# A two-block kernel (global filter by DFT, then an MLP mixer): filter loads spread over three queues, the rounding's addition on Pool, the first token weights folded in two halves, and the next batch's head between a batch's last products

## Chip, cores, metric

One core of a Trainium2 chip. The metric is the device time of one execution in microseconds, as a median of several runs of the same kernel. Kernels that were timed together ran on the same chip. A ratio is the mean time of one kernel's runs over that of the other's of the same rounds, so it is not quite the ratio of the medians quoted beside it. Engines are written as the profile has them: PE (matmul), PEld (weight load), DVE, ACT, POOL, SP; "SPq" and "ACTq" are DMA issues of those engines.

## The reference

```python
X = np.fft.rfft(x, axis=1)                                # x: (8, 3008, 256)
y = np.fft.irfft(X * (filt_r + 1j * filt_i)[None], n=3008, axis=1).astype(np.float32)
xt = y.transpose(0, 2, 1)
h = np.maximum(xt @ w_tok1, 0) @ w_tok2                   # token mixing, 3008 -> 256 -> 3008
u = y + h.transpose(0, 2, 1)
out = (u + np.maximum(u @ w_ch1, 0) @ w_ch2).astype(np.float32)   # channels, 256 -> 1536 -> 256
```

The four weights arrive as float64 and are rounded to float32 on the chip.

## The kernel before

Before the matmul work of batch 0 can run at full rate there are three stages. **A**: twelve units of the first DFT of batch 0, beside them twelve pieces of the first token weights, each rounded on ACT and DVE and then *folded* with the inverse DFT on PE. **B**: sixteen chunks of two units each: second DFT, product with the filter on DVE, inverse DFT. **C**: sixteen roundings of the second token weights. After that PE works on the mixer of a batch, with the DFT of the following batches between. The parts that the change touches:

```python
def filt_load(c):                      # nine (for c = 0: twelve) DMAs, all on SP
    for src, i, p0 in ((filt_r, 0, 0), (filt_r, 0, HALF), (filt_i, 1, HALF)):
        nc.sync.dma_start(...)         # and two reversed pieces
# filt_keep(c): the arranged filter goes to DRAM;  filt_again(c): later batches fetch it with two DMAs

def rounded(st, n, parts):             # float64 words in st -> float32
    top, rest = pp.tile(...), pp.tile(...)                     # two buffers each
    nc.scalar.activation(out=top, in_=hi_f, func=AF.Copy, scale=2.0 ** -112)
    nc.vector.tensor_scalar(out=top_i, ...)                    # shift
    nc.vector.scalar_tensor_tensor(out=top_i, in0=hi, ...)     # sign
    nc.vector.tensor_scalar(out=rest_i, in0=top_i, ...)        # exponent
    nc.vector.scalar_tensor_tensor(out=rest, in0=lo, ...)
    for src, dst in parts:
        nc.vector.tensor_tensor(out=dst, in0=src(top), in1=src(rest), op=ALU.add)

# ... main part
for i, _ in enumerate(dft(GROUPS[0])):
    if i < A // 2:
        next(convert)                  # rounding i; then the load of a later piece, on POOL
    if 0 < i <= A // 2:
        w1_fold(i - 1)                 # the fold of the step before
# ... 16 + 2 further roundings, then mix(b): token_hidden, u of part 0, 36 items of products
```

In the stretches of the traces that were read here each engine runs its instructions in the order in which the program emits them; a DMA issue waits in its engine's order like any other.

Of the kernel before, what the change touches and what calls it, by code (L numbers as in the profile page):

```python
# [17 lines left out]
B = 8  # L18
N = 3008
N1 = 47  # L20
N2 = 64
# [92 lines left out]
def kernel(  # L114
# [24 lines left out]
    f_d = nc.dram_tensor("f_tmp", (K2 // KC, P, 2, KC, D), FP32, kind="Internal").ap()  # L139

# [41 lines left out]
    def filt_load(c):  # L182
        t, k0 = filts[c % FB], c * KC
        for src, i, p0 in ((filt_r, 0, 0), (filt_r, 0, HALF), (filt_i, 1, HALF)):
            nc.sync.dma_start(t[p0:p0 + A, i], raw(src, k0, [[64 * D, A], [D, KC], [1, D]]))
            lo = p0 + 32
            if k0 == 0:
                nc.sync.dma_start(t[lo:lo + A, i, 0, :], raw(src, 32, [[64 * D, A], [1, D]]))
            k = max(k0, 1)

            for j0, n in ((0, 16), (16, A - 1 - 16)):
                nc.sync.dma_start(t[lo + j0:lo + j0 + n, i, k - k0:KC, :],  # L192
                                  raw(src, 64 * (j0 + 1) - k, [[64 * D, n], [-D, k0 + KC - k], [1, D]]))

    def filt_parts(c):
        t = filts[c % FB]
        return (t[:, 0], f_d[c, :, 0]), (t[HALF:P, 1], f_d[c, HALF:P, 1])

    def filt_keep(c):
        for sb, dr in filt_parts(c):  # L200
            nc.sync.dma_start(dr, sb)

    def filt_again(c):
        for sb, dr in filt_parts(c):
            nc.sync.dma_start(sb, dr)
# [3 lines left out]
    stages = ([(t4p, "t4")] * (A // 2) + [(up, "u")] * 2  # L209
              + [((t2p, "t2"), (t3p, "t3"))[i % 2] for i in range(TC * N2 // NG + JT - 2)])  # L210
# [5 lines left out]
    def rounded(st, n, parts):  # L216

        words = [st.bitcast(t).rearrange("p (n w) -> p n w", w=2)[:, 0:n] for t in (U32, FP32)]
        lo, hi, hi_f = words[0][:, :, 0], words[0][:, :, 1], words[1][:, :, 1]

        top = pp.tile([P, 512], FP32, tag="p1", name="top")[:, 0:n]
        rest = pp.tile([P, 512], FP32, tag="p2", name="rest")[:, 0:n]
        top_i, rest_i = top.bitcast(U32), rest.bitcast(U32)


        nc.scalar.activation(out=top, in_=hi_f, func=AF.Copy, scale=2.0 ** -112)
        nc.vector.tensor_scalar(out=top_i, in0=top_i, scalar1=3, scalar2=None, op0=ALU.logical_shift_left)
        nc.vector.scalar_tensor_tensor(out=top_i, in0=hi, scalar=0x80000000, in1=top_i,  # L228
                                       op0=ALU.bitwise_and, op1=ALU.bitwise_or)
        nc.vector.tensor_scalar(out=rest_i, in0=top_i, scalar1=0xFF800000, scalar2=None, op0=ALU.bitwise_and)  # L230

        nc.vector.scalar_tensor_tensor(out=rest, in0=lo, scalar=2.0 ** -52, in1=rest, op0=ALU.mult, op1=ALU.mult)  # L232
        for src, dst in parts:
            nc.vector.tensor_tensor(out=dst, in0=src(top), in1=src(rest), op=ALU.add)
# [41 lines left out]
    def wc1_load(i):  # L276
        c, q = divmod(i, DC // 512)
        st = stage(512)
        for g in range(CB):
            nc.gpsimd.dma_start(st[ts(g, CW)], moe_w_ch1[ds((g * DH + c) * CW, CW), ts(q, 512)])  # L280
        yield
        rounded(st, 512, [(lambda v: v, wc1[:, c, ts(q, 512)])])

    def wc2_load(i):
        st = stage(512)
        nc.gpsimd.dma_start(st.rearrange("p (j d) -> p j d", d=D),
                            moe_w_ch2[ts(i, 2 * P), :].rearrange("(j p) d -> p j d", p=P))
        yield

        def tile_of(dh):  # L290
            return lambda v: v.rearrange("p (j g e i) -> p e j g i", j=2, e=DH, i=CW)[:, dh]

        a11, a12, s4, na22, s3, s2, s1 = (wc2[:, i, n, :] for n in range(7))

        rounded(st, 512, [(tile_of(dh), wc2[:, i, n].rearrange("p j (g i) -> p j g i", i=CW))
                          for dh, n in ((0, slice(0, 2)), (1, slice(4, 7, 2)))])
        add = nc.gpsimd.tensor_tensor
        nc.gpsimd.tensor_scalar(out=na22, in0=s1, scalar1=-1.0, scalar2=None, op0=ALU.mult)
        add(out=s1, in0=s3, in1=s1, op=ALU.add)
        add(out=s3, in0=a11, in1=s3, op=ALU.subtract)  # L300
        add(out=s2, in0=s1, in1=a11, op=ALU.subtract)
        add(out=s4, in0=a12, in1=s2, op=ALU.subtract)  # L302
# [5 lines left out]
    def weights():  # L308

        steps = ([w1_load(i) for i in range(A // 2)] + [w2_load(i) for i in range(TC * N2 // NG)]  # L310
                 + [wc1_load(c * (DC // 512)) for c in range(DH)]
                 + [f(i) for f, i in LAST])
        n1 = A // 2
        for s in steps[0:AHEAD]:
            next(s)
        yield
        for i, s in enumerate(steps[0:n1]):
            next(s, None)
            if i + AHEAD < n1 + 2:
                next(steps[i + AHEAD])  # L320
            yield
        for s in steps[n1 + 2:n1 + AHEAD]:
            next(s)
        for i, s in enumerate(steps[n1:]):
            next(s, None)
            if n1 + i + AHEAD < len(steps):
                next(steps[n1 + i + AHEAD])
# [26 lines left out]
    def dft(bs):  # L354
# [12 lines left out]
        def load(c):  # L367
# [6 lines left out]
            if first:  # L374
                filt_load(c)
                if c:
                    filt_keep(c - 1)
            else:
                filt_again(c)
# [38 lines left out]
        for k in range(K2 + 1):  # L418
# [6 lines left out]
            if k == K2 and first:  # L425
                filt_keep(K2 // KC - 1)
# [74 lines left out]
    def finish(b, m, ut, po):  # L501
# [24 lines left out]
        for h in range(2):  # L526
            n = min(4, (w - h * HALF + HALF) // P)
            for e in range(2):
                for g in range(CB):
                    nc.gpsimd.dma_start(rows[g, e, :, ds(h * A + 4 * m, n)], blocks[ts(g, CW), h, e, 0:n])  # L530

    def mix(b, next_ready, convert):
        h1 = token_hidden(b)
        wait = []
        uts, pos, hhs, sms = {}, {}, {}, {}

        def u_part(m, dh):
            if dh == 0:
                uts[m] = up.tile([P, DH, 512], FP32, tag="u", name="u")
            u_unit(b, m, h1, uts[m], dh)  # L540
            if dh == DH - 1 and b + 1 < B:
                wait.append(m)

        def step():
            if next_ready():
                for c in wait:
                    t4_load(b + 1, c)
                wait.clear()

        for dh in range(DH):  # L550
            u_part(0, dh)
        items = [(m, jp) for m in range(MT) for jp in range(JP)]
        for i in range(len(items) + 1):
            for half in range(2):
                next(convert, None)
                if i < len(items):
# [3 lines left out]
                    hidden(uts[m], 2 * jp + half, width(m), hhs[i])  # L560
                    if half == 1:
                        sms[i] = sums(hhs[i], width(m))
                        if m + 1 < MT and jp in (2, 3):
                            u_part(m + 1, jp - 2)
                if half == 1 and i >= 1:
                    m, jp = items[i - 1]
                    products(m, jp, hhs.pop(i - 1), sms.pop(i - 1), pos.setdefault(m, []))
                    if jp == JP - 1:
                        finish(b, m, uts[m], pos[m])
                step()  # L570
                yield

    with tc.manual_schedule():
# [5 lines left out]
        next(convert)  # L579
        for i, _ in enumerate(dft(GROUPS[0])):  # L580
# [3 lines left out]
            if i < A // 2:  # L584
                next(convert)
            if 0 < i <= A // 2:
                w1_fold(i - 1)
        for c in range(A // TC4):
            t4_load(0, c)
        for _ in range(TC * N2 // NG + DH):  # L590
            next(convert)
        for bs, after in zip(GROUPS, GROUPS[1:] + ((),)):
# [41 lines left out]
```

## Time and profile before

| | before |
|---|---|
| median of 4 runs | 2755.6 us (2750.8 to 2756.4) |
| PE busy | 95% |
| A: first product of B starts | 65.1 us |
| B: its last product starts | 174.5 us |
| C: second token weights ready | 221.2 us |
| first mixer product (`ps_pg`) | 231.0 us |
| last product ends / span ends | 2733.5 / 2752.2 us |

The prediction below quotes the views that carry the reading: busy shares, slices, stretches, the ring of stage A, the SP queue of stage B and the waits of PE. Two more views belong to it. First the engine table cut at the ends of B and C (length, then busy time of PE, PEld, DVE, ACT and POOL with the number of instructions, granted clock, DMA share, GB/s):

```profile
65.11:175.62 110.51, 63.56 (x129) 33.11 (x127) 53.37 (x128) 11.99 (x32) 1.25 (x3) 0.55 0.61 177
176.47:221.25 44.78, 23.46 (x96) 19.96 (x96) 42.01 (x97) 9.33 (x17) 10.99 (x21) 0.73 0.73 238
```

In B no compute engine is full; SP's issues take 5.8 of each 6.9 us (the prediction shows them). In C DVE is busy 42.0 of 44.8 us. One rounding of C in the timeline (start, length, engine and line, operation, the idle time before it):

```profile
177.43 0.55 DVE L228 SCALAR_TENSOR_TENSOR top<-st,top 128x376 uint32<-128x376 uint32 x1
...
178.98 0.86 DVE L234 TENSOR_TENSOR w<-top,rest 128x368 f32<-128x368 f32 x2
```

The two additions take 0.86 us together.

### The profile page before, as it was taken

What the parts mean: (1) busy time and instruction counts of PE and PEld (TensorE: products, weight loads), DVE (VectorE), ACT (ScalarE), POOL (GpSimd) and SP (SyncE); (2) the same over time, 40 slices, a digit from 0 to 9 for tenths busy, and PEclk for the clock granted to TensorE, in tenths of its full rate; (3) what the DMA queues carried; (4) which work ended last, traced back from release to release, by engine and by line L of the source; (5) the groups of instructions that cost most, each with busy time, mean ns of one, the idle gap of its engine ahead of it and who ended that gap; (6) DMA issues with size and microseconds to landing.
All of it is one profiled execution on the core that took longest, in us unless ns stands there. A gap on an engine that the chain in (4) does not pass through costs nothing.

```text
span 2752.2 us, 25374 instructions
## 1 busy us (share of the span) xinstructions
PE 2609.9 (95%) x9112; PEld 1677.0 (61%) x9112; DVE 1213.1 (44%) x2306; ACT 529.0 (19%) x941; POOL 471.7 (17%) x873
## 2 busy tenths in 40 slices
PE   4567999999999999999999999999999999999997
PEld 1344655576666666675666665676666766676665
DVE  5468377522336356322235455431345343323333
ACT  3113222112222122112221112211212111111111
POOL 2014211121121112121112111210211211221122
PEclk9568999999999999999999999999999999999998
DMA  7665344412233222202232222211322211000000
GB/s 220 182 210 173 123 141 128 130 34 87 76 101 93 63 88 63 82 15 84 83 108 78 67 87 74 71 31 59 99 73 76 69 47 31 23 15 8 8 16 15
DMA packets 163140, 222.31 MB, mean 81 GB/s; under 512 B 29764, under 2 KB 100967, under 8 KB 163015
## 3 DMA queue, kind: packets, MB, share of 16 engines
q1 hardware_dynamic: 92519, 126.90, 15.4%
q0 software_dynamic: 29760, 43.31, 6.3%
q10 hardware_dynamic: 40736, 50.48, 5.4%
q8 instruction: 73, 1.20, 0.2%
q14 instruction: 52, 0.43, 0.1%
HBM read 139.30 MB, written 81.26 MB: 80 GB/s over the span
## 4 chain that ended last, share of the span: by engine, by line
PE 91%; DVE 3%; DMA 3%; SPq 1%; issue 1%; ACT 1%; POOL 0%; ACTq 0%; DVEq 0%; POOLq 0%
PE ps_pg L467 35%; PE ps_po L498 31%; PE ps_acc L455 6%; PE ps_acc L441 5%; PE ps_b L386 4%; PE ps_acc L402 4%; PE ps_acc L460 3%; PE ps_b L349 3%; DMA t<-z_tmp 1%; DMA g_tmp<-t 1%; SPq L192 0%; DVE top L228 0%; DVE rest L232 0%; DMA wai_t<-wait_t 0%; DVE rest L230 0%
## 5 line engine op out<-in xcount | busy, mean ns | idle before, releaser
L467 PE MATMUL ps_pg<-u,wc 128*128 128x512 f32 (+1 forms) x2304 | 1046.9, 584 | 0.0
L530 POOL DMA_DIRECT2D out_dram<-r x768 | 416.0, 550 | 2047.5 <-DVE r L523 1943.6
L467 PEld LDWEIGHTS ps_pg<-u,wc 128*128 128x128 f32 x2304 | 436.4, 190 | 421.3 <-issue 401.7
L469 ACT ACTIVATE hh<-ps_pg 128x512 f32<-128x512 f32 (+1 forms) x576 | 338.8, 588 | 1512.9 <-PE ps_pg L467 1512.9
L498 PE MATMUL ps_po<-t,wc 128*128 128x256 f32 (+1 forms) x2304 | 582.4, 375 | 0.0
L482 DVE TENSOR_TENSOR t<-hh 128x512 f32<-128x512 f32 (+1 forms) x288 | 195.7, 679 | 875.0 <-ACT hh L469 873.9
L498 PEld LDWEIGHTS ps_po<-t,wc 128*128 128x128 f32 x2304 | 438.4, 190 | 50.0
L498 PE MATMUL ps_po<-hh,wc 128*128 128x256 f32 (+1 forms) x1728 | 461.1, 376 | 2.2 <-POOL wc L302 2.2
L498 PEld LDWEIGHTS ps_po<-hh,wc 128*128 128x128 f32 x1728 | 322.3, 190 | 119.4 <-issue 88.4
L394 DVE TENSOR_TENSOR p<-ps_b,filt 128x512 f32<-128x512 f32 (+1 forms) x144 | 86.2, 598 | 368.9 <-PE ps_b L386 329.6
L455 PE MATMUL ps_acc<-w,h 128*128 128x512 f32 (+1 forms) x384 | 180.5, 593 | 25.8 <-ACT h L444 19.5
L386 PE MATMUL ps_b<-t,wb 96*128 96x512 f32 (+1 forms) x288 | 137.0, 559 | 48.2 <-DMA t<-z_tmp 33.7
L441 PE MATMUL ps_acc<-t,w 128*128 128x256 f32 x768 | 169.6, 383 | 8.7 <-DMA t<-g_tmp 8.7
L441 PEld LDWEIGHTS ps_acc<-t,w 128*128 128x128 f32 x768 | 147.6, 192 | 29.5 <-issue 9.4
L402 PE MATMUL ps_acc<-p,wi 128*96 128x512 f32 (+1 forms) x320 | 152.8, 562 | 5.1 <-issue 2.8
L462 DVE COPY u<-ps_acc 128x512 f32<-128x512 f32 (+1 forms) x96 | 65.3, 680 | 195.4 <-PE ps_acc L460 194.0
L455 PEld LDWEIGHTS ps_acc<-w,h 128*128 128x128 f32 x384 | 72.1, 191 | 113.6 <-issue 82.8
L407 ACT COPY t<-ps_acc 96x512 f32<-96x512 f32 (+1 forms) x160 | 79.5, 497 | 286.4 <-PE ps_acc L402 286.4
L460 PEld LDWEIGHTS ps_acc<-wai,t 128*128 128x128 f32 x768 | 101.4, 192 | 44.8 <-issue 44.8
L484 DVE TENSOR_TENSOR t<-t,hh 128x256 f32<-128x256 f32 (+1 forms) x288 | 121.4, 421 | 9.9
L483 DVE TENSOR_TENSOR t<-t,hh 128x256 f32<-128x256 f32 (+1 forms) x288 | 120.8, 419 | 9.8
L386 PEld LDWEIGHTS ps_b<-t,wb 96*128 96x128 f32 x288 | 56.6, 203 | 112.0 <-issue 47.7
(50 smaller groups left out, 1160.5 us busy)
## 6 DMA issues: line engine op xcount, KB each, us to landing
z_tmp<-t ACTq DMA_DIRECT2D x96, 256.0 KB
t<-z_tmp SPq DMA_DIRECT2D x128, 192.0 KB
g_tmp<-t ACTq DMA_DIRECT2D x128, 192.0 KB
t<-g_tmp SPq DMA_DIRECT2D x48, 512.0 KB
x<-in_x_dram SPq DMA_DIRECT2D x176, 128.0 KB
out_dram<-r POOLq DMA_DIRECT2D x704, 32.0 KB, 1.8
filt<-f_tmp SPq DMA_DIRECT2D x64, 256.0 KB
filt<-f_tmp SPq DMA_DIRECT2D x64, 128.0 KB
```

The costliest lines, as they stand in the source:

```text
L386: nc.tensor.matmul(ps, wbs[k // WC][:, k % WC, :], t2s[k // KC][:, k % KC], start=True, stop=True)
L402: nc.tensor.matmul(ps[0:KR], wis[k // WC][:, k % WC, :], prods.pop(k), start=True, stop=True)
L441: nc.tensor.matmul(acc[:, t, :], w1[:, a, ts(t, P)], t4[b, a // TC4][:, a % TC4, :], start=(a == 0 and t == 0), stop=(a == A - 1 and t == ...
L455: nc.tensor.matmul(ps[:, 0:w], h1[:, t, ts(dh, P)], w2[:, t, ds(m * 512, w)], start=(t == 0), stop=False)
L460: nc.tensor.matmul(ps[:, ds(q * P, n)], t4[b, c][:, r, ts(dh, P)], wai[:, 0:n], start=False, stop=(q == 3))
L467: nc.tensor.matmul(ps[:, 0:w], wc1[:, c, ts(jt, P)], ut[:, c, 0:w], start=(c == 0), stop=(c == DH - 1))
L469: nc.scalar.activation(out=hh[:, jt % 2, 0:w], in_=ps[:, 0:w], func=AF.Relu)
L482: v(out=t[:, 0:2, 0:hw], in0=hh[:, :, hw:w], in1=hh[:, 0, 0:w].rearrange("p (s n) -> p s n", s=2), op=ALU.subtract)
L483: v(out=t[:, 2, 0:hw], in0=t[:, 1, 0:hw], in1=hh[:, 0, 0:hw], op=ALU.add)
L484: v(out=t[:, 3, 0:hw], in0=t[:, 2, 0:hw], in1=hh[:, 1, 0:hw], op=ALU.subtract)
L498: nc.tensor.matmul(po[i][:, j, 0:hw], wc2[:, jp, n, :], mov, start=(jp == 0 and j == 0), stop=(jp == JP - 1 and j == len(parts) - 1))
L530: nc.gpsimd.dma_start(rows[g, e, :, ds(h * A + 4 * m, n)], blocks[ts(g, CW), h, e, 0:n])
```

## The change

Its intent: take SP's issues out of stage B, take the additions off DVE, spread the token weights' folding over A and B, fill PE's waits at the batch boundaries, and issue the last outputs from three queues. The core of the diff:

```diff
-    def filt_load(c):
+    def filt_load(c, queues):
...
+        for q, (src, i, p0) in zip(queues, ((filt_r, 0, 0), (filt_r, 0, HALF), (filt_i, 1, HALF))):
+            q.dma_start(...)
-            if first: filt_load(c); if c: filt_keep(c - 1)      # shortened
-            else: filt_again(c)
+            filt_load(c, (nc.sync, nc.scalar, nc.gpsimd) if first else (nc.sync,) * 3)
+    early = [(up, "u")] * 2 + [(tp, "t")] * 2 + [(rp, "r")] * 2   # staging of w2: other pools than t2, t3
...
-            nc.vector.tensor_tensor(out=dst, in0=src(top), in1=src(rest), op=ALU.add)
+            nc.gpsimd.tensor_tensor(out=dst, in0=src(top), in1=src(rest), op=ALU.add)
...
-            if i < A // 2:
-                next(convert)
-            if 0 < i <= A // 2:
-                w1_fold(i - 1)
+            if i % 2 == 1 and i < NXC or i % 3 == 2 and NXC < i <= NXC + 3 * (A // 4):
+                next(convert)
+                w1_fold(next(folds))                             # the fold of this very rounding
...
+                        if more and i == n - 2: h1s[b + 1] = token_hidden(b + 1)   # in mix, shortened
+                        if more and i == n - 1: u_part(b + 1, 0, 0)
+                elif more and half == 0: u_part(b + 1, 0, 1)
...
+                    q = (nc.sync, nc.scalar, nc.gpsimd)[(h * 8 + e * 4 + g) % 3] if last else nc.gpsimd
```

The temporaries of the roundings that stand before batch 0's mixer also move, from the pool that B's products with the filter use to that of the hidden tiles, with two buffers as before. And batch 0's token product now stands before the two roundings of the channel weights, no longer behind them.

More of the change, by code (lines that the diff above doesn't have):

```diff
@@ L137 @@
     g_d = nc.dram_tensor("g_tmp", (B, K2, KR, D), FP32, kind="Internal").ap()
-    f_d = nc.dram_tensor("f_tmp", (K2 // KC, P, 2, KC, D), FP32, kind="Internal").ap()
     def pool(name, bufs, **kw):
@@ L180, in raw @@
         return bass.AP(tensor=src.tensor, offset=src.offset + row * D, ap=ap)
-    def filt_load(c):
+    def filt_load(c, queues):
         t, k0 = filts[c % FB], c * KC
-        for src, i, p0 in ((filt_r, 0, 0), (filt_r, 0, HALF), (filt_i, 1, HALF)):
-            nc.sync.dma_start(t[p0:p0 + A, i], raw(src, k0, [[64 * D, A], [D, KC], [1, D]]))
+        for q, (src, i, p0) in zip(queues, ((filt_r, 0, 0), (filt_r, 0, HALF), (filt_i, 1, HALF))):
+            q.dma_start(t[p0:p0 + A, i], raw(src, k0, [[64 * D, A], [D, KC], [1, D]]))
             lo = p0 + 32
             if k0 == 0:
-                nc.sync.dma_start(t[lo:lo + A, i, 0, :], raw(src, 32, [[64 * D, A], [1, D]]))
+                q.dma_start(t[lo:lo + A, i, 0, :], raw(src, 32, [[64 * D, A], [1, D]]))
             k = max(k0, 1)
             for j0, n in ((0, 16), (16, A - 1 - 16)):
-                nc.sync.dma_start(t[lo + j0:lo + j0 + n, i, k - k0:KC, :],
-                                  raw(src, 64 * (j0 + 1) - k, [[64 * D, n], [-D, k0 + KC - k], [1, D]]))
-    def filt_parts(c):
-        t = filts[c % FB]
-        return (t[:, 0], f_d[c, :, 0]), (t[HALF:P, 1], f_d[c, HALF:P, 1])
-    def filt_keep(c):
-        for sb, dr in filt_parts(c):
-            nc.sync.dma_start(dr, sb)
-    def filt_again(c):
-        for sb, dr in filt_parts(c):
-            nc.sync.dma_start(sb, dr)
-    stages = ([(t4p, "t4")] * (A // 2) + [(up, "u")] * 2
-              + [((t2p, "t2"), (t3p, "t3"))[i % 2] for i in range(TC * N2 // NG + JT - 2)])
+                q.dma_start(t[lo + j0:lo + j0 + n, i, k - k0:KC, :],
+                            raw(src, 64 * (j0 + 1) - k, [[64 * D, n], [-D, k0 + KC - k], [1, D]]))
+    early = [(up, "u")] * 2 + [(tp, "t")] * 2 + [(rp, "r")] * 2
+    late = [(t2p, "t2"), (t3p, "t3"), (t2p, "t2"), (t3p, "t3"), (t2p, "t2")]
+    stages = [(t4p, "t4")] * (A // 2) + early * 3 + late * 2
     def stage(n):
@@ L214, in stage, with rounded @@
         return where.tile([P, n], I64, tag=tag, name="st")
-    def rounded(st, n, parts):
+    def rounded(st, n, parts, late=False):
         words = [st.bitcast(t).rearrange("p (n w) -> p n w", w=2)[:, 0:n] for t in (U32, FP32)]
         lo, hi, hi_f = words[0][:, :, 0], words[0][:, :, 1], words[1][:, :, 1]
-        top = pp.tile([P, 512], FP32, tag="p1", name="top")[:, 0:n]
-        rest = pp.tile([P, 512], FP32, tag="p2", name="rest")[:, 0:n]
+        if late:
+            top = pp.tile([P, 512], FP32, tag="p1", name="top")[:, 0:n]
+            rest = pp.tile([P, 512], FP32, tag="p2", name="rest")[:, 0:n]
+        else:
+            both = hp.tile([P, 2, 512], FP32, tag="hh", name="both")
+            top, rest = both[:, 0, 0:n], both[:, 1, 0:n]
         top_i, rest_i = top.bitcast(U32), rest.bitcast(U32)
@@ L274, in w2_load, with wc1_load @@
         rounded(st, n, [(both, dst[:, :, :, ds(g * NG, NG)]), (some(w, 1), w2[:, t, ds(w * P + g * NG, NG)].unsqueeze(1))])
-    def wc1_load(i):
+    def wc1_load(i, late=True):
         c, q = divmod(i, DC // 512)
@@ L281, in wc1_load @@
         yield
-        rounded(st, 512, [(lambda v: v, wc1[:, c, ts(q, 512)])])
+        rounded(st, 512, [(lambda v: v, wc1[:, c, ts(q, 512)])], late)
     def wc2_load(i):
@@ L295, in wc2_load @@
         rounded(st, 512, [(tile_of(dh), wc2[:, i, n].rearrange("p j (g i) -> p j g i", i=CW))
-                          for dh, n in ((0, slice(0, 2)), (1, slice(4, 7, 2)))])
+                          for dh, n in ((0, slice(0, 2)), (1, slice(4, 7, 2)))], True)
         add = nc.gpsimd.tensor_tensor
@@ L310, in weights, with load @@
         steps = ([w1_load(i) for i in range(A // 2)] + [w2_load(i) for i in range(TC * N2 // NG)]
-                 + [wc1_load(c * (DC // 512)) for c in range(DH)]
-                 + [f(i) for f, i in LAST])
-        n1 = A // 2
-        for s in steps[0:AHEAD]:
-            next(s)
+                 + [wc1_load(c * (DC // 512), False) for c in range(DH)])
+        n = len(steps)
+        steps += [f(i) for f, i in LAST]
+        loads = iter(steps)
+        def load(k):
+            for _, s in zip(range(k), loads):
+                next(s)
+        load(AHEAD)
         yield
-        for i, s in enumerate(steps[0:n1]):
+        for i, s in enumerate(steps):
             next(s, None)
-            if i + AHEAD < n1 + 2:
-                next(steps[i + AHEAD])
-            yield
-        for s in steps[n1 + 2:n1 + AHEAD]:
-            next(s)
-        for i, s in enumerate(steps[n1:]):
-            next(s, None)
-            if n1 + i + AHEAD < len(steps):
-                next(steps[n1 + i + AHEAD])
+            load(i != n - 1)
             yield
@@ L373, in load @@
                 nc.sync.dma_start(wis[g], wi_d[:, ts(g, WC), :])
-            if first:
-                filt_load(c)
-                if c:
-                    filt_keep(c - 1)
-            else:
-                filt_again(c)
+            filt_load(c, (nc.sync, nc.scalar, nc.gpsimd) if first else (nc.sync,) * 3)
             t2s[c] = t2p.tile([KR, KC, nb, D], FP32, tag="t2", name="t2")
@@ L424, in dft @@
                 bi_unit(k - 1)
-            if k == K2 and first:
-                filt_keep(K2 // KC - 1)
             yield
@@ L529, in finish, with u_part @@
                 for g in range(CB):
-                    nc.gpsimd.dma_start(rows[g, e, :, ds(h * A + 4 * m, n)], blocks[ts(g, CW), h, e, 0:n])
-    def mix(b, next_ready, convert):
-        h1 = token_hidden(b)
-        wait = []
-        uts, pos, hhs, sms = {}, {}, {}, {}
-        def u_part(m, dh):
-            if dh == 0:
-                uts[m] = up.tile([P, DH, 512], FP32, tag="u", name="u")
-            u_unit(b, m, h1, uts[m], dh)
-            if dh == DH - 1 and b + 1 < B:
-                wait.append(m)
-        def step():
-            if next_ready():
-                for c in wait:
-                    t4_load(b + 1, c)
-                wait.clear()
-        for dh in range(DH):
-            u_part(0, dh)
+                    last = b == B - 1 and m == MT - 1
+                    q = (nc.sync, nc.scalar, nc.gpsimd)[(h * 8 + e * 4 + g) % 3] if last else nc.gpsimd
+                    q.dma_start(rows[g, e, :, ds(h * A + 4 * m, n)], blocks[ts(g, CW), h, e, 0:n])
+    h1s, uts = {}, {}
+    def u_part(b, m, dh):
+        if dh == 0:
+            uts[b, m] = up.tile([P, DH, 512], FP32, tag="u", name="u")
+        u_unit(b, m, h1s[b], uts[b, m], dh)
+    def mix(b, next_ready, convert):
+        wait = [0]
+        pos, hhs, sms = {}, {}, {}
+        more = b + 1 < B
         items = [(m, jp) for m in range(MT) for jp in range(JP)]
-        for i in range(len(items) + 1):
+        n = len(items)
+        for i in range(n + 1):
             for half in range(2):
                 next(convert, None)
-                if i < len(items):
+                if i < n:
                     m, jp = items[i]
@@ L559, in mix @@
                         hhs[i] = hp.tile([P, 2, 512], FP32, tag="hh", name="hh")
-                    hidden(uts[m], 2 * jp + half, width(m), hhs[i])
+                    hidden(uts[b, m], 2 * jp + half, width(m), hhs[i])
                     if half == 1:
@@ L563, in mix @@
                         if m + 1 < MT and jp in (2, 3):
-                            u_part(m + 1, jp - 2)
+                            u_part(b, m + 1, jp - 2)
+                            if jp == 3:
+                                wait.append(m + 1)
+                        if more and i == n - 2:
+                            h1s[b + 1] = token_hidden(b + 1)
+                        if more and i == n - 1:
+                            u_part(b + 1, 0, 0)
+                elif more and half == 0:
+                    u_part(b + 1, 0, 1)
                 if half == 1 and i >= 1:
@@ L568, in mix @@
                     if jp == JP - 1:
-                        finish(b, m, uts[m], pos[m])
-                step()
+                        finish(b, m, uts[b, m], pos[m])
+                if more and next_ready():
+                    for c in wait:
+                        t4_load(b + 1, c)
+                    wait.clear()
                 yield
@@ L579 @@
         next(convert)
+        folds = iter(range(A // 2))
         for i, _ in enumerate(dft(GROUPS[0])):
@@ L583 @@
                     nc.scalar.dma_start(t, src)
-            if i < A // 2:
+            if i % 2 == 1 and i < NXC or i % 3 == 2 and NXC < i <= NXC + 3 * (A // 4):
                 next(convert)
-            if 0 < i <= A // 2:
-                w1_fold(i - 1)
+                w1_fold(next(folds))
+        assert next(folds, None) is None
         for c in range(A // TC4):
             t4_load(0, c)
-        for _ in range(TC * N2 // NG + DH):
+        for _ in range(TC * N2 // NG):
             next(convert)
+        h1s[0] = token_hidden(0)
+        for _ in range(DH):
+            next(convert)
+        for dh in range(DH):
+            u_part(0, 0, dh)
         for bs, after in zip(GROUPS, GROUPS[1:] + ((),)):
```

## The prediction

> **What bounds the kernel now.** I read the page's busy shares first, then its slices, then the same engine table cut into stretches, then the chain of waits and the order of instructions inside each stretch. The page says where the end is set:
>
> ```profile
> PE 2609.9 (95%) x9112; PEld 1677.0 (61%) x9112; DVE 1213.1 (44%) x2306; ACT 529.0 (19%) x941; POOL 471.7 (17%) x873
> PE   4567999999999999999999999999999999999997
> PEclk9568999999999999999999999999999999999998
> ```
>
> One slice is 68.8 us. TensorE (PE) is full from the fifth slice to the last but one; only the start and the end have holes. The change keeps PE's work, so it can win only the start, the small holes between batches, and the tail. The stretches (columns as in the page: PE, PEld, DVE, ACT, POOL busy, then granted clock, DMA share, GB/s):
>
> ```profile
> 50.00:100.00 50.00, 30.30 (x56) 14.12 (x56) 27.84 (x60) 9.27 (x20) 0.00 (x0) 0.63 0.52 154
> 100.00:150.00 50.00, 29.08 (x59) 15.19 (x58) 24.17 (x59) 5.15 (x14) 0.00 (x0) 0.50 0.63 184
> 200.00:250.00 50.00, 32.27 (x102) 19.82 (x102) 42.30 (x87) 12.82 (x22) 22.43 (x42) 0.80 0.60 175
> 250.00:300.00 50.00, 50.00 (x167) 30.15 (x166) 32.45 (x62) 17.69 (x30) 14.33 (x26) 1.00 0.44 143
> ```
>
> The start has three stages; the instruction order gives their ends.
> Stage A (to 65 us): batch 0's twelve first-DFT units, each beside one rounding of the float64 token weights and one fold of them on PE. The chain in order of time turns in this ring:
>
> ```profile
> 34.33 0.44 DVE top L227
> ...
> 36.70 0.70 DVE w L234
> 37.54 1.10 PE ps_po L254 x2
> 38.64 0.87 PE ps_acc L349 x2
> ```
>
> The ring returns at 44.53, and it holds two units: 3.5 us a unit, which is the five VectorE (DVE) operations of one rounding (0.44+0.70+0.44+0.70+0.70 = 2.98) and gaps. Note that the fold uses the rounding of the step before.
> Stage B (65.1 to 175.6 us, 110.5 us): 16 chunks of two units, 6.9 us a chunk. PE waits for t<-z_tmp, and that load stands last in the SP queue behind the filter loads:
>
> ```profile
> 110.06 0.32 SPq L371 DMA_DIRECT2D wb<-wb_t  x1
> ...
> 113.59 0.71 SPq L192 DMA_DIRECT2D filt<-in_filt_i_dram  x2
> 114.34 0.84 SPq L201 DMA_DIRECT2D f_tmp<-filt  x2
> 115.23 0.59 SPq L382 DMA_DIRECT2D t<-z_tmp  x1
> 115.92 0.41 SPq L371 DMA_DIRECT2D wb<-wb_t  x1
> ```
>
> Fourteen issues take 5.8 us; the rest of the 6.9 us is a short wait. SP's issue rate bounds this stage.
> Stage C (176.5 to 221.2 us): 16 roundings of the second token weights, DVE back to back, 44.7/16 = 2.8 us each. PE finishes the token product at 208 and then waits 14.7 us for it.
>
> **What the Trainium skill says.** (1) DMA: Bandwidth & Descriptors, "Issuing engines are not separate DMA queues": using several issuing engines saves only the sequencer's issue time. Here that is what stage B lacks: SP is full while the DMA share is 0.61. (2) GPSIMD Engine Reference, 3.1 "Elementwise": a two-input add takes about 2.6 cycles an element at 1.2 GHz, some twice DVE's. Before's Pool adds of 128x128 take 0.46 us when alone, so an estimate for 128x512 is 0.46 + 384 x 2.6/1.2 ns = 1.3 us, against DVE's 0.70; no run shows that size yet. (3) SBUF — State Buffer, "Who interferes with whom": a DVE instruction with two SBUF inputs, or in a two-port mode, locks out a Pool instruction that reads SBUF, and the reverse. The trace agrees that they disturb each other (the first line is a Pool add beside roundings, the second one alone; the third a DVE operation beside Pool, the fourth the same alone):
>
> ```profile
> 241.17 0.78 POOL L300 TENSOR_TENSOR wc<-wc 128x128 f32<-128x128 f32 x1
> 249.53 0.46 POOL L300 TENSOR_TENSOR wc<-wc 128x128 f32<-128x128 f32 x1
> 240.81 0.83 DVE L228 SCALAR_TENSOR_TENSOR top<-st,top 128x512 uint32<-128x512 uint32 x1
> 244.33 0.69 DVE L228 SCALAR_TENSOR_TENSOR top<-st,top 128x512 uint32<-128x512 uint32 x1
> ```
>
> (4) TensorE: Matmul & The Clock Gate, Part 1: after an idle window of about 3.4 us PE runs at half rate. Stage B shows granted clocks of 0.50 to 0.63, and a fold's pair takes 2.04 us cold (54.46) and 1.10 warm (37.54). But a gap of 3.25 us at 27 us left it warm.
>
> **Part by part.**
> *Filter loads on three queues, no copies kept.* Per chunk SP keeps wb, wi, three filter loads and t: about 6 issues, 2.5 us instead of 5.8. SP no longer bounds B. What comes next is DVE: four operations a unit, 1.71 us from unit to unit inside a chunk (112.34, 114.05), and PE cold, 1.87 (118.33 to 120.20). I take 1.85 us a unit; 32 units would be 59 us, which alone would win about 50 us. Later batches re-read filters with 9 issues a chunk where there were 2; SP then needs about 5.4 us of some 10 us a chunk with two batches, and the loads run two chunks ahead: hidden.
> *First token weights in two halves.* Six roundings stay in A, six move into B. But in the new loop the rounding and **its own fold** stand in the same step; before, the fold lagged by a step. PE runs its instructions in the program's order throughout the trace, so it now waits for the whole rounding before it may start the next unit. In A, from fold to fold, from before's durations: fold 0.95, two units 0.87 each, copy of the second 0.7, its store's issue and the gap 0.5 + 0.5, ACT's top 0.7, four DVE operations 2.35, Pool's add 1.35, waits between engines 0.4: about 9.2 us warm, 10.8 cold, instead of 7.0 for the same two units. Fold 0 stays at 21.8 us (wai_t's landing); five periods later the last fold is at 68 to 76, mid 72, against 63.3. Pool's three filter loads of chunk 0 stand behind that add, so the first product of B is usable some 4 us later, at 76 against 66. A: **+8 us** (the ring hides some of the difference at its ends).
> In B a step with a fold costs: the unit's product 1.25, its DVE work 1.71, the rounding 2.35 and its add 1.4, the fold 1.8 cold, waits and ACT 0.6: 9.1 us instead of 1.85. Six of them are 55 us, 26 plain ones 48: 103 us, against 110.5. B: **-8 us**. So nearly all that SP's relief gives is taken by PE's new waits.
> *Add on Pool, C.* DVE keeps four operations: 0.40+0.58+0.40+0.58 = 1.95 us an item instead of 2.8. Pool gets per item an add of 368 elements (estimate 0.98 us with the page's slope, up to 1.6 as its input is read with a step of 47 elements), one of 8 elements (0.2) and a DMA issue of 0.54 (1.95 for the four-piece channel weights): 1.8 to 2.4 us, with DVE's port in the way of each add. The two temporaries have two buffers, so the ring of top, DVE and add also allows only about 2.4 us. I take 2.8 +- 0.4 and 2 us for the last add: **+2 us**, a wash. The preloaded weights do not help, since DVE's rounding, not the transfer, set this stage.
> Afterwards h1's relu no longer stands behind the channel weights' roundings (1.3 us), and the 2.2 us that PE waited for POOL wc L302 should go as Pool's order improves: **-3 us**. Start in sum: +8 -8 +2 -3 = -1 us.
> *Head between the last products.* All PE waits after 250 us:
>
> ```profile
> PE ps_b L386 <- DVE p L396: 5.8, 2, 3.1
> PE ps_acc L455 <- DVE u L462: 5.5, 7, 0.8
> PE ps_acc L455 <- ACT h L444: 4.8, 7, 0.7
> ```
>
> The last two are seven batch boundaries, 1.5 us each. Products now stand between the token product, its relu and the two u parts, so all of it is covered: **-10 us**. The loads of the next batch's t4 come in time: at the tightest boundary they are issued at 535.6 to 539 us and the token product would start near 563.
> *Last outputs on three queues.*
>
> ```profile
> 2736.92 8.65 POOL L530 DMA_DIRECT2D out_dram<-r  x16 [21.47 <-DVE r L523]
> ```
>
> A third of these on each queue end after about 2.9 us: **-5 us**, landing unchanged.
> Sum: 2756 - 1 - 10 - 5 = 2740 us; I shade it to 2738, since stage A may stay warm.
>
> **Rivals.** (a) *The queues were the whole problem*: B falls to 60-75 us, A does not grow, and the time is about 2695. For it: SP is full in B, and DVE and PE have room. Against: the order of the fold, which is plain in the code; PE must wait. (b) *Pool becomes the bound of C*: 3.3 us and more an item, C grows by 10 us, end near 2755. For it: both engines want one port without a break, and the 0.46 to 0.78 us above; against: before's Pool is busy in only 22 of the 50 us at 200 to 250. (c) *The transfers bound A and B*: the DMA share is 1.0 around 5 to 25 us, so folds would be hidden behind loads; but from 50 us on it is 0.2 to 0.65, so I doubt it. (d) *Filter re-reads stall the later batches*: each PE wait in mid-kernel would add up; a few us at most, as loads run 20 us ahead.
>
> **Range and chances.** Good ends of the terms: PE warm in A and B (start -22), heads -10, tail -6: 2718. Bad ends: cold PE (+10), C +10, tail -4, heads -8: 2764. Rival (a) leaves a tail of chance below. 8 in 10: 2708 to 2762. Faster by over 2% means below about 2702: 0.10; slower by over 2% needs +55 us, for which I see no source: 0.01.
>
> **What would show it.** In the changed profile: folds in A 9 to 11 us apart, each with PE idle 4 us or more before it and released by Pool's add; in B six gaps of about 9 us between units and otherwise near 1.9; SP in B with idle time; C's items 2.4 to 3.2 us apart, with DVE operations beside adds longer than 0.55; PE idle from 250 us to the tail 6 us instead of 16.5; the last output issue some 3 us after the transposes. I am wrong if PE's wait before folds is short, or if B's plain units stay at 3 us because loads still come late.

## The result, and the profile after

The changed kernel takes 2755.1 us (median of 4; 2752.6 to 2755.7), before 2755.6 us. The ratio is 1.0 with a 95% interval of 0.9983 to 1.0017: the same. The prediction had 2738. The time lies in its range, but the gain that it forecast is not there.

Slices and granted clock of the page after, one digit for 68.8 us:

```profile
PE   4466999999999999999999999999999999999997
PEclk8668999999999999999999999999999999999999
```

The start got longer (its four slices read 4, 4, 6, 6 instead of 4, 5, 6, 7). The same two stretches as before, B and C by the changed kernel's own ends:

```profile
78.24:190.20 111.96, 62.21 (x141) 32.62 (x139) 66.47 (x152) 19.19 (x44) 36.81 (x61) 0.65 0.50 139
190.99:243.90 52.91, 25.83 (x98) 20.65 (x98) 50.59 (x66) 9.79 (x18) 44.97 (x59) 0.69 0.65 201
```

B is as long as before, although its DMA share fell from 0.61 to 0.50; C grew by 8.1 us, and DVE is *busier* in it with 31 instructions fewer. Stage A in PE's timeline (in square brackets PE's idle time before the instruction and what released it):

```profile
33.84 2.07 PE L245 MATMUL ps_po<-w,wai_t 128*128 128x512 f32 x2 [5.54 <-POOL w L225]
35.71 1.91 PE L338 MATMUL ps_acc<-x,wa 128*128 128x512 f32 x2
37.41 1.85 PE L338 MATMUL ps_b<-x,wa 128*128 128x512 f32 x2
44.89 2.08 PE L245 MATMUL ps_po<-w,wai_t 128*128 128x512 f32 x2 [5.63 <-POOL w L225]
...
101.94 2.08 PE L245 MATMUL ps_po<-w,wai_t 128*128 128x512 f32 x2 [4.81 <-POOL w L225]
```

One fold and two units take 11.05 us, of which PE waits 5.6 us for Pool's addition; before, two folds and two units took 7.0. Every fold takes some 2.07 us, which the prediction calls cold; before, most folds of A took 1.10. The last line is a fold of B. There PE stands 37.3 us in six such waits, the longest 10.7; in the kernel before it stood 42.4 us in B for loads (33.7 for t, 8.7 for wi), and of the wait for t 2.6 are left. So one wait took the other's place. Now C in the timeline:

```profile
193.63 1.99 POOL L225 TENSOR_TENSOR w<-both 128x368 f32<-128x368 f32 x2 [15.90 <-DVE both L223]
193.84 1.71 DVE L219 SCALAR_TENSOR_TENSOR both<-st,both 128x376 uint32<-128x376 uint32 x1
195.57 0.57 POOL L253 DMA_DIRECT2D st<-in_moe_w_tok_dram  x1
195.98 0.55 DVE L223 SCALAR_TENSOR_TENSOR both<-st,both 128x376 f32<-128x376 uint32 x1
196.62 2.00 POOL L225 TENSOR_TENSOR w<-both 128x368 f32<-128x368 f32 x2 [0.48 <-DVE both L223]
```

DVE's second operation starts 0.2 us after Pool's addition and ends just before Pool's next instruction: 1.71 us instead of 0.55. "Busy" here is waiting. The ring is 3.0 us an item: Pool's two additions 1.99, then DVE's third and fourth operation 0.36 and 0.55, and gaps.

The waits of PE after the start, of the changed kernel (line, releaser, us in total, times, longest):

```profile
PE ps_b L370 <- DVE p L380: 5.5, 2, 2.7
PE ps_po L480 <- POOL wc L293: 0.7, 1, 0.7
```

The fourteen boundary waits are gone. Where the kernels stand at the marks of the start (us, profiled runs; e6, e10 and e11 are experiments below):

| | before | after | e6 | e10 | e11 |
|---|---|---|---|---|---|
| B's first product starts | 65.1 | 78.2 | 67.4 | 53.2 | 69.2 |
| B's last product starts | 174.5 | 189.1 | 137.0 | 136.4 | 137.5 |
| first mixer product starts | 231.0 | 253.6 | 192.5 | 199.5 | 194.8 |
| span | 2752.2 | 2753.2 | 2711.1 | 2700.9 | 2695.8 |

From the first mixer product to the end of the last, before took 2733.49 - 231.02 = 2502.5 us and after takes 2737.42 - 253.56 = 2483.9. So the start lost 22.5 us, the full stretch won 18.6, and the tail (end of the last product to the end of the span) went from 18.7 to 15.8 us: 22.5 - 18.6 - 2.9 = +1.0, the difference of the two profiled spans.

### The profile page after: what moved, and what is told of

The parts are those of the page before. It is cut to its first block, busy times and chain, and to the rows that moved or that the text cites. A ratio compares the mean times of both kernels' runs of the same rounds, so it can differ in the third digit from the quotient of the medians.

```text
span 2753.2 us, 26044 instructions
## 1 busy us (share of the span) xinstructions
PE 2603.7 (95%) x9112; PEld 1677.2 (61%) x9112; DVE 1214.5 (44%) x2244; ACT 528.6 (19%) x941; POOL 558.1 (20%) x973
## 4 chain that ended last, share of the span: by engine, by line
PE 90%; DVE 4%; issue 2%; DMA 2%; POOL 1%; ACT 0%; SPq 0%; ACTq 0%; DVEq 0%; POOLq 0%
PE ps_pg L449 35%; PE ps_po L480 31%; PE ps_acc L437 6%; PE ps_acc L423 5%; PE ps_acc L386 4%; PE ps_b L370 4%; PE ps_acc L442 3%; PE ps_b L338 2%; DVE both L219 1%; POOL w L225 1%; DMA filt<-in_filt_r_dram 1%; DVE both L223 0%; DMA filt<-in_filt_i_dram 0%; DMA x<-in_x_dram 0%; DVE both L221 0%
## 5 line engine op out<-in xcount | busy, mean ns | idle before, releaser
L515 POOL DMA_DIRECT2D out_dram<-r x757 | 409.8, 550 | 2028.8 <-DVE r L505 2008.0
L386 PE MATMUL ps_acc<-p,wi 128*96 128x512 f32 (+1 forms) x320 | 147.3, 544 | 10.7 <-DVE p L381 4.3
L490 DVE TENSOR_TENSOR u<-ps_po,u 128x256 f32<-128x256 f32 (+3 forms) x240 | 113.0, 517 | 8.6 <-PE ps_po L480 1.4
L442 PE MATMUL ps_acc<-wai,t 128*128 128x128 f32 (+1 forms) x768 | 101.9, 276 | 0.0
```

What stands on the lines that cost most here:

```text
L386: nc.tensor.matmul(ps[0:KR], wis[k // WC][:, k % WC, :], prods.pop(k), start=True, stop=True)
L442: nc.tensor.matmul(ps[:, ds(q * P, n)], t4[b, c][:, r, ts(dh, P)], wai[:, 0:n], start=False, stop=(q == 3))
L515: q.dma_start(rows[g, e, :, ds(h * A + 4 * m, n)], blocks[ts(g, CW), h, e, 0:n])
```

## The experiments

The theory at this point: the fold of the same step makes PE wait for the whole rounding, and that eats what the queues gave; in C Pool's addition holds DVE. Rival 1: filter data comes late through the three queues, and that sets A and B. Rival 2: conflicts of Pool and DVE are the whole cause. All kernels below gave correct results; times are medians.

**1. One step of lag (e1).** To the changed kernel:

```diff
+            if due:
+                w1_fold(next(folds)); due = False
             if i % 2 == 1 and i < NXC or ...:
                 next(convert)
-                w1_fold(next(folds))
+                due = True
```

> The changed kernel with one edit: a fold is emitted one step after its rounding, as in the kernel before. Theory (PE's in-order wait for the rounding of the same step ate the relief of the queues): folds of the first stage 5 to 7 us apart instead of 10.7, the first stage shorter by 15 us or more, the second stage 70 to 85 us instead of 112, the third unchanged at some 53 us; time 2695 to 2720. Rival 1 (the filter loads now come late through three queues, so the data sets the second stage): it stays above 100 us and the time within 15 us of 2755. Rival 2 (Pool's adds and DVE block each other everywhere): first and second stage within 10 us of the changed kernel's, time within 15 us.

Measured: 2737.4 us, ratio to before 0.9939 (0.9924 to 0.9954). The direction was right, the size was not: -17 us, where 35 to 60 had been expected. Its folds are still 9.2 to 9.7 us apart in A, with PE waiting before each:

```profile
34.07 2.08 PE L245 MATMUL ps_po<-w,wai_t 128*128 128x512 f32 x2 [4.26 <-POOL w L225]
43.48 2.08 PE L245 MATMUL ps_po<-w,wai_t 128*128 128x512 f32 x2 [3.92 <-POOL w L225]
```

Rounding j+1 stands on ACT behind the copy of a unit that stands on PE behind fold j. So with one fold for two units, a lag of one step leaves one closed ring. (In the kernel before, with one fold a unit, the same lag gives two rings that run interleaved.) Rival 1 was not excluded yet.

**2. The addition back on DVE (e2).** `nc.gpsimd.tensor_tensor` becomes `nc.vector.tensor_tensor` in `rounded`, and nothing else.

> The changed kernel with the rounding's addition back on DVE, folds still in the rounding's own step. Theory: the third stage falls from 53 to 45 us (no Pool add holds DVE's two-input operation for 1.2 us), each of the twelve fold waits is some 0.5 us shorter, so first stage -3, second -3: time 2738 to 2745. Rival 2 (port conflicts are the main cause): -30 us or more, time below 2725. Rival 1: only the third stage moves, 2745 to 2748.

Measured: 2739.6 us, 0.9947 (0.9932 to 0.9962), as expected. B's first product comes 2.6 us earlier, B is 6 us shorter (its last product starts at 180.3 us instead of 189.1), and the second token weights are ready 46.3 us after that instead of 54.9. Rival 2 falls: the addition's place on Pool costs some 15 us with the waits that it feeds, not everything. (This run does not part the conflict from the addition's own length, for 512 elements 1.25 us on Pool and 0.70 on DVE.)

**3. Both (e3).**

> Both edits. Theory: the gains add, first stage -15 to -20, second -30 to -40, third -8: time 2685 to 2712, faster than both kernels. Rival 1: 2740 or more.

Measured: 2718.6 us, 0.9866 (0.985 to 0.9883). The two gains add (-17 and -15 give -36 here), but the first product of B still starts at 70.9 us and the time missed the expected interval, since the ring was still closed.

**4. A full lag (e10), and with the addition on DVE (e9).** The fold of the previous rounding is emitted after the *next* rounding:

```diff
                 next(convert)
-                w1_fold(next(folds))
+                if due:
+                    w1_fold(next(folds))
+                due = True
+        w1_fold(next(folds))          # the last one, after the loop
```

> The changed kernel, with the fold of the previous rounding emitted only after the next rounding has been emitted (so two to three steps after its own). The one-step lag won only 17 us and its folds stayed 9.3 us apart, because rounding j+1 stands on ACT behind the copy of a unit that stands on PE behind fold j: still one ring. Theory: with the next rounding already under way the ring is open; folds of the first stage at most 6 us apart on average, the first product of the second stage at 55 to 63 us instead of 78, the second stage 75 to 90 us instead of 112; time 2700 to 2722 (third stage still 53 us). Rival (loads through the queues or the transfers set both stages): as with the one-step lag, 2733 to 2740.

> The same with the rounding's addition on DVE. Theory: third stage 45 us, no add to wait for; time 2685 to 2708, the best so far. Rival: no better than 2715 (the lag and the add together gave 2718.6 with a one-step lag).

Measured: e10 2704.8 us, 0.9822 (0.9804 to 0.984); e9 2697.1 us, 0.9787 (0.9772 to 0.9802). With only the folds' place in the program's order changed, the changed kernel is 50 us faster. B's first product starts at 53.2 us instead of 78.2 (five folds now stand before it instead of six) and its last at 136.4 instead of 189.1. In e10 PE waits at most 2.8 us before a fold of A and not at all before those of B:

```profile
29.23 1.13 PE L245 MATMUL ps_po<-w,wai_t 128*128 128x512 f32 x2 [0.17 <-POOL w L225]
42.41 1.13 PE L245 MATMUL ps_po<-w,wai_t 128*128 128x512 f32 x2 [2.23 <-POOL w L225]
...
66.87 1.92 PE L245 MATMUL ps_po<-w,wai_t 128*128 128x512 f32 x2
```

Five of its twelve folds take 1.0 to 1.13 us, the others 1.5 to 2.1; what went is above all the waits.

Loads, queues and transfers are the same as in the changed kernel, so rival 1 falls. e9 against e10 gives Pool's addition its price once the ring is open: 8 us by time. In the traces C is 8.0 us shorter in e9 (46.9 us from B's last product to the second token weights, 54.9 in e10), but A and B together are 3.5 us longer with the additions on DVE, and u comes later after C: the first mixer product starts only 1.7 us earlier (197.8 against 199.5). Another 3.4 us of the two spans' 5.2 lie in the full stretch. So where the 8 us are won is not shown.

**5. The filter loads alone (e6).** The kernel before with `filt_load` on three queues and without the copies.

> The kernel before with only the filter loads changed: three queues, no copies kept, later batches read the filters again. Folds, additions, head and tail as before. Theory: SP's issues were the bound of the second stage, so it falls from 110 us to 60 to 75 us, first and third stage within 3 us of before, time 2710 to 2722. Rival (the second stage is held by the landing of its data, whatever queue issues it): it stays above 95 us, time above 2738.

Measured: 2715.4 us, 0.9853 (0.9837 to 0.9869), within the expectation. B of this kernel:

```profile
67.44:138.00 70.56, 52.28 (x129) 27.97 (x127) 53.08 (x128) 12.32 (x33) 22.31 (x42) 0.68 0.66 185
```

70.6 us instead of 110.5, with A and C unchanged within 3 us. SP's issues were the bound of B, and the larger number of filter DMAs of the later batches costs nothing that shows: PE's waits after the start are those of before. The run makes two edits at once: it spreads the loads and drops the copies to DRAM (two of SP's fourteen issues a chunk, 0.84 of the 5.8 us). No run parts them.

**6. The head alone (e4).** The kernel before with the new `mix`.

> The kernel before with only the next batch's head moved between a batch's last products. Theory: the seven boundary waits of 1.5 us (10.3 us together) go, PE idle between 250 us and the tail falls from 16.5 to about 6 us, time -10 us: 2743 to 2748. Rival (the head takes a new wait in exchange, for the u copies or the output banks): within 3 us of before.

Measured: 2742.2 us, 0.9959 (0.9944 to 0.9974), so 11 us. In the trace the full stretch is 2720.29 - 235.34 = 2485.0 us, 17.5 less than before; that run's start was 4 us later than that of before, without a cause in the edit. The stretch is the better measure: it is 2502.3 to 2502.6 us in three of the traces with the old head (before, e5, e6; in e7, where Pool's additions add waits, it is 2506.9) and 2482 to 2486 in the nine with the new one. The rival (a new wait in exchange) falls.

**7. The tail alone (e5).**

> The kernel before with only the last tile's outputs on three queues. Theory: the issues of the last outputs end 5.9 us earlier, but in the changed kernel the span ran on for 9.6 us after the last issue instead of 6.6, so -3 us: 2750 to 2754. Rival (landing and the end of the program take the rest): within 1 us of before.

Measured: 2746.9 us, 0.9968 (0.9956 to 0.9981), 9 us (5 to 12), more than expected. From the end of the last product to the end of the span it takes 11.4 us; before 18.7, in the changed kernel 15.8. The issues explain 5.9 us of it. The rest is in the stretch after the last issue, in which the trace shows no compute instruction and, beyond the first two microseconds, no output transfer: 5.3 us here, 6.6 before, 9.6 in the changed kernel. What ends it stays open. The seven kernels made from the changed one have the 9.6 us too, so of the 7.3 us that e5's trace wins in the tail only 2.9 are found there.

**8. Pool's addition alone (e7).** The kernel before with `nc.gpsimd` in `rounded`.

> The kernel before with only the rounding's addition moved to Pool. Theory (Pool's add holds DVE's two-input operation until it ends): third stage 45 to 53 us with DVE's second operation at 1.7 us instead of 0.55, so +8; the first stage +0 to +4, as its two interleaved rings each get 0.6 us longer but DVE has less to do: time 2760 to 2770. Rival (the move relieves DVE, its intent): third stage 35 us or less, time below 2748.

Measured: 2794.7 us, 1.0146 (1.0129 to 1.0164): 38 us slower. The sign was right, the size off by far: from B's last product to the first u it takes 76.8 us instead of 48.0, the roundings coming in pairs of 8.4 us, and A is 6.0 us longer. The profile suggests two causes for the pairs. DVE is held as in the changed kernel, here in its first operation, which is one of one input:

```profile
191.17 1.63 DVE L227 TENSOR_SCALAR top<-top 128x376 uint32<-128x376 uint32 x1 [2.97 <-ACT top L226]
...
196.74 0.55 POOL L262 DMA_DIRECT2D st<-in_moe_w_tok_dram  x1 [3.87 <-issue]
```

And Pool sits idle for 3.9 us before a weight load, with additions behind it in its order; what it waits for, the profile doesn't name. In this kernel's staging, from the code, the load of a piece takes a tile that the next roundings still read; the changed kernel's separate staging tiles remove that, and its Pool waits only 0.5 us an item. That second cause is read from code and trace; no run isolates it.

**9. Candidates for a better version (e11, e12).** e11 is the changed kernel with its two costly parts undone: addition on DVE, and all folds in A, one unit and one step after their roundings, as before. e12 also puts eight of C's sixteen roundings between units of B (`if i >= 16 and i % 4 == 0: next(convert)`).

> The changed kernel with the two parts that cost time undone: the rounding's addition on DVE, and all token folds in the first stage, one step after their roundings, as before. Kept: filter loads on three queues, early staging, head, tail. Theory: the parts add (queues -40, head -11, tail -9 as each measured alone): 2690 to 2702. Rival (the parts overlap, as all three relieve the same path): above 2705.

> The same, with eight of the sixteen second-weight roundings put between the units of the second stage. PE waits for none of them until the token product's u, and DVE works 55 of that stage's 70 us, so part of each 2.8 us falls into DVE's gaps. Theory: second stage 74 to 84 us, third stage 22 us instead of 45: time 2672 to 2690. Rival (DVE is full there, so the work is only moved): within 4 us of the version without it.

Measured: e11 2697.9 us, 0.979 (0.9775 to 0.9805), as expected; e12 2705.5 us, 0.9817 (0.9801 to 0.9833), a miss. B of e11 and of e12:

```profile
69.22:138.70 69.48, 50.89 (x129) 27.36 (x127) 53.04 (x128) 12.37 (x33) 21.10 (x39) 0.72 0.65 183
71.46:163.60 92.14, 55.57 (x129) 31.93 (x127) 73.68 (x176) 16.01 (x40) 25.81 (x47) 0.61 0.60 171
```

Eight roundings (some 2.8 us each, 22.4 us) lengthen B by 22.7 us. DVE had 16 us without work in e11's B, and none of it was used. The waits of PE for DVE in B, first of e11 and then of e12, show how:

```profile
PE ps_acc L386 <- DVE p L381: 5.4, 11, 1.1
PE ps_acc L386 <- DVE p L381: 34.3, 16, 4.9
```

In DVE's order a unit's own products stand behind the rounding, and PE waits up to 4.9 us for them. Whether a finer mixing would do better was not tried. e11 and e9 beat both kernels by 2.1% (both intervals reach past 0.98, so whether by more than 2% is open) and are equal to each other, so folding in two halves won nothing here.

By time the parts add up. Measured alone on the kernel before: queues -40 (e6), head -11 (e4), tail -9 (e5), together -60, and e11 has -58. On top of that the changed kernel has the fold in its own rounding's step, +50 (changed kernel against e10), and Pool's addition, +8 (e10 against e9): zero. Two cautions. The split of the 58 depends on the order: undone first, the addition is worth 15 (e2), and the lag then 44 (e9 against e2). And that -60 comes so near to -58 is partly luck: in e11's trace the start is 36.2 us shorter than before's (e6 alone: 38.5), the full stretch 17.3 (e4 alone: 17.5, of which its longer start hid 4) and the tail 2.9 (e5 alone: 7.3). The early staging was in every kernel made from the changed one and was not tested alone.

## Why the prediction was right or wrong

- **What bounds the kernel, and what could move: right.** Start, boundaries and tail are all that changed. SP's issues as the bound of B: right (e6).
- **The fold's wait: the right mechanism, and the predicted ring.** A ring of 9.2 us warm to 10.8 cold was forecast, 10.4 to 11.05 came, every fold cold. (The 10.8 has no working: with the cold steps of before's trace, 1.83 us for a fold and 1.71 for a unit, the same sum gives 11.8; in three of the five rounds the second unit was faster again.) The forecast waits of 4 us or more, released by Pool's addition, are there (5.5 to 5.7). In B a fold and two plain units were worked out as 9.1 + 2 x 1.85 = 12.8 us; measured 12.0 to 13.7.
- **The step that failed is the sum of the start, "+8 -8 +2 -3 = -1 us"; it is +22.5 (first mixer product).** Term by term: A is +13.1 instead of +8 (the working itself had 76 against 66, which is 65.1 in the trace, and was then shaded; the folds were cold throughout, and wai_t landed 1 us later). B's term, "103 us, against 110.5", is +1.5 (112.0 us) instead of -8: the first fold of B comes 13.6 us after the last of A, the chain of waits naming the filters of chunk 0 landing to 85 us, and the plain units of the second half took 33.7/16 = 2.1 us instead of 1.85, with waits for DVE, ACT and t that the estimate had left out. By the prediction's own figures the stretch to the sixth fold of B holds 6 steps with a fold and 10 plain ones, 73 us, and took 77.1; the 16 plain units after it 30 us, and took 34.8 to the end of B. The 1.85 us a unit was low without folds too: e6's B takes 70.6 us, 2.2 a unit, where 59 were worked out. The waits before the folds, which the prediction had, are the bulk: 37.3 us of B.
- **C's term, "2.8 +- 0.4 ... a wash", failed at its size: +8.1 us.** An item takes 3.0 us, and 3.9 where Pool also issues four pieces. The estimate had Pool's main addition at 0.98 to 1.6 us and the small one at 0.2; they measured 1.52 and 0.53. And the two engines' times were treated as mostly overlapping, while DVE's operation waits for nearly the whole addition. This was rival (b) of the prediction, at nearly its full 10 us.
- **"Afterwards ... -3 us" did not come.** h1's relu is early, but u's products then wait for the last additions on Pool (4.2 us) and for DVE behind the channel weights (1.9 us); 9.7 us from the ready second token weights to the first mixer product, 9.8 before.
- **The head, "-10 us", was too small: -17.5 us in the full stretch (e4; -18.6 in the changed kernel).** The listed waits (10.3 us) are less than what a boundary cost, since the products around a wait take longer too, and that is booked as busy. At the boundary after batch 0 the token product, both u parts and the first mixer product take 29.85 us of PE's time in before (574.31 to 604.16) and 20.72 + 2.61 + 2.61 + 1.72 = 27.66 in e4: 2.19 us. Seven of these are 15.3; 2 us stay open.
- **The tail, "-5 us, landing unchanged"**: -5.9 at the issues, but the end of the program moved by itself: -2.9 in the changed kernel's trace, -9 by time in e5.
- Rival (a), the queues as the whole problem with A not growing and the time at about 2695, was wrong for the changed kernel, where A grew by 13.1 us; its number is that of e11 (2697.9), which has the queues, head and tail without the fold's wait. Rival (c) shows only at the filters of chunk 0, before the first fold of B; (d) did not happen.

So the prediction named the cancelling mechanism and missed that it would cancel everything: A was set below its own working, B left out the waits between plain units, and C took two engines as overlapping that hold each other up. That the time came out only 17 us above the forecast is partly luck: the start was 23.5 us worse than forecast, the head 8.6 us better.

## What to carry to other kernels

Where one engine must consume what a chain of other engines makes, emit the consumer after the *next* link of the chain is already under way; a lag that suffices with one consumer per step can be too short when the steps are regrouped. An engine that looks idle is no free place for an operation if its work holds up the engine that is to be relieved, as here: look at how long that engine's operations get, and at everything that stands behind the moved operation in the new engine's order. Measure the parts of a compound change alone before judging it: here the queues, the head and the tail were worth 58 us together, and the fold's place and the addition's took them back.

## What the Trainium skill lacked or had wrong

- DMA: Bandwidth & Descriptors, "Issuing engines are not separate DMA queues": it says that several issuing engines save only the sequencer's time and that this is usually small beside the transfer. The first half agrees; here that time was 5.8 of 6.9 us a chunk, so not small, and spreading it, with the copies dropped, won 40 us (e6).
- GPSIMD Engine Reference, 3.1: the slope agrees: 0.46 us at 128 and 1.25 us at 512 elements are 2.06 ns, at the 1.2 GHz that the page gives 2.5 cycles an element (2.6 on the page). Missing: the time of a very short addition (8 elements, 0.53 us, where the same two points give 0.21; 0.17 on DVE).
- SBUF — State Buffer, "Who interferes with whom": agrees. A DVE operation with two inputs went from 0.55 to 1.71 us, each time until about the end of Pool's addition. A one-input `tensor_scalar` went from 0.35 to 1.63 us (e7), which the page allows in a two-port mode; the trace does not show the mode.
- TensorE: Matmul & The Clock Gate, Part 1: the idle window of about 3.4 us is not enough to tell here which folds are cold. Waits of 5.5 us kept every fold at 2.07 us, but in e9 a wait of 2.36 us behind two warm units was followed by a fold of 2.08 us, while in e10 one of 2.23 us was followed by 1.13; and in the kernel before the granted clock fell from 1.00 to 0.50 at 53 us, with no wait before a product over 2.1 us in the 20 us before. What decides is not shown.
- No page that was looked at says why the stretch from the last output's issue to the end of the span differs between kernels: 5.3, 6.6 and 9.6 us in e5, the kernel before and the changed kernel.
